# A spectral filter beside an S2-MLP: when the first and third group are turned, and when two layer norms are applied

## The chip, the cores and the metric

The kernel runs on one core of one Trainium2 chip. A core has five engines with a queue each: TensorE (PE in the profile, with its weight loads as PEld) multiplies matrices, VectorE (DVE) and ScalarE (ACT) work elementwise and move results out of PSUM, GpSimd (POOL) works elementwise on data in SBUF, and SyncE (SP) issues the DMA transfers. The metric is device time of one execution in microseconds; the median of several executions counts.

## The reference

`x` is 2048 tokens by 448 channels, `w1` and `w2` are 448 by 448, `w3` is 448 by 1792, `w4` is 1792 by 448, and the spectral weights are 2048 by 225 complex numbers.

```python
def _A_ref(x, w_r, w_i):
    X = rfft2(x, axes=(-2, -1)) * (w_r + 1j * w_i)
    return irfft2(X, s=(S, D), axes=(-2, -1))

def _B_ref(x, w1, w2, w3, w4):
    h = gelu(layernorm(x) @ w1)
    c = D // 4
    g0 = jnp.pad(h[:, :, 0*c:1*c], ((0, 0), (1, 0), (0, 0)))[:, :S, :]   # shift +1
    g1 = jnp.pad(h[:, :, 1*c:2*c], ((0, 0), (0, 1), (0, 0)))[:, 1:, :]   # shift -1
    g2 = jnp.pad(h[:, :, 2*c:3*c], ((0, 0), (2, 0), (0, 0)))[:, :S, :]   # shift +2
    g3 = jnp.pad(h[:, :, 3*c:   ], ((0, 0), (0, 2), (0, 0)))[:, 2:, :]   # shift -2
    hs = jnp.concatenate([g0, g1, g2, g3], axis=-1) @ w2
    x1 = x + hs
    return x1 + gelu(layernorm(x1) @ w3) @ w4

xn = layernorm(x)
return x + _A_ref(xn, w_r, w_i) + _B_ref(xn, w1, w2, w3, w4)
```

Gelu is the tanh form. The MLP branch gets `xn` and normalizes it once more.

## The kernel before

**Data.** The 16 blocks b of 128 rows (`xb(b)`, the tiles xt0 to xt3) lie in four groups of four blocks (`GRP`). The groups are numbered 0 to 3 in the order in which they are worked. Every product of fp32 values is made of three fp16 products: each operand is split into a high part and the remainder (`hi`, `lo`), and hi·hi, hi·lo and lo·hi are summed in PSUM. ACT usually writes the high part, and DVE the low part from it.

**PSUM.** `bank(tag, ...)` gives one of two PSUM banks of each of four tags: "mm", "tr", "acc" and "sp". A bank is free again when its last reader is done.

**First phase, 0 to about 75 us.** The steps for a group g are these.

- `norm1(g, engines)` takes mean and variance (L309, L310) and a first estimate of the reciprocal root on DVE (L333 to L338), and applies both to the four blocks in place (L345 on ACT or L348 on the engine named in the list, one entry per block). It returns `refine` and `scales`, small POOL instructions (L356 to L376) that make the exact per-row scales; `gsc` is needed by the gelu.
- `T1(g)` turns the group: for each of four column tiles t, `turn_pe` transposes four 128 by 128 pieces on PE into one bank (L396), and `turn_copy` writes the high (L406, ACT) and low part (L407, DVE) to `xT`.
- `w1_in` multiplies with w1 (L446; 11 products of 448 columns per block, a block being called a unit here), and `w1_unit` takes the gelu (L465, ACT), splits it into `hs` (L466 ACT, L467 DVE) and has SP transpose it by DMA into `h` (L470).
- `w2_tile(b)` multiplies the shifted pieces of h with w2 (L486; 12 products) and adds to x with L488 on DVE.
- `ln2(blocks, engines, pins)` is the second layer norm: statistics on DVE, the subtraction of the mean (L509 on ACT or L511 on the engine named), a reciprocal root from small DVE instructions, the split into hi (L519, ACT) and lo (L520 and L522, DVE) in a stage tile `y`, and a DMA transpose on SP (L524) into `x2mem`, from where the third layer reads.

The weights w1, w2, w3 and w4 are scaled by powers of two (`powers`: sums of squares by L243 on ACT, L248 on DVE, one product L254, L256 to L261 on DVE) and split. For w3 the split is eight pairs of L284 (ACT) and L285 (DVE). The raw w3 comes by SP (L218); its last quarter is issued behind the eighth h transpose of group 1. The raw w4 (L229) is loaded by SP into space of `x2mem`.

**Main phase.** `mlp` runs eight unit groups G of 256 rows, each with seven pairs fp: `front` (L417 products with w3, gelu L731, split L733 on ACT and L734 on DVE) and `back` (L753 products with w4). Between them stand the steps of the spectral branch. `do_fold` loads two blocks of x, normalizes them on ACT (L548) and folds them on POOL (L554, L557). `step1_in` splits the fold (L564 ACT, L565 DVE), and `step1` multiplies (L574). Then come the column transform, the weights (`wc`, loaded at L619), and the inverse.

**What sets the order.** A scheduler fixes the order of instructions on each engine from the program, the dependences and its own timing model. `behind(key)` adds an order by hand: the instructions within it are issued behind those recorded under the key in `after`. `LATE` gives the pair (G, fp) behind whose split the instructions of the last `ln2` stand, `FOLD` and `PACE` do so for folds and step1, and `WMAX` for maxima over the spectral weights.

Of the kernel before, what the change touches and what calls it, by code (L numbers as in the profile page):

```python
# [13 lines left out]
F16 = mybir.dt.float16  # L14
# [5 lines left out]
S, D, DF, F = 2048, 448, 225, 1792  # L20
# [3 lines left out]
CS = {b: 4 * g + i for b, (g, i) in WHERE.items()}  # L24
PASS = ((0, 0), (0, 1), (1, 0))
SHIFT = [1, -1, 2, -2]
WARM = 25
ZPRE = 2.0 ** -7
UPRE = 2.0 ** -3
VPRE = 2.0 ** -3  # L30
# [3 lines left out]
FOLD = [(0, 5), (1, 0), (1, 1), (1, 3), (1, 4), (1, 6), (2, 0), (2, 2)]  # L34
PIN = [("a3",), ("a3",), ("a3",), ("a3",)]
WMAX = [(1, 4), (1, 5), (1, 6), (2, 0), (2, 1), (2, 2), (2, 3), (2, 4)]
LATE = [(0, 6), (0, 6), (1, 2), (1, 2)]
HS = 3
INV, LAG = 4, 2
EVAC, FILL = 0, 100000  # L40
# [81 lines left out]
def body(tc, nc, x, wf, w1, w2, w3, w4, c_g, c_n, c_small, out):  # L122
    V, A, P, T, SY = nc.vector, nc.scalar, nc.gpsimd, nc.tensor, nc.sync
# [28 lines left out]
    def bank(tag, name):  # L152
        return ps.tile([128, 512], F32, tag=tag, bufs=2, name=name)
# [10 lines left out]
    def xb(b):  # L164
        g, i = WHERE[b]
        return xt[g][:, i]
# [4 lines left out]
    def stage(name, n, side, dtype=F32):  # L171
        t = pw.tile([128, 1808], F32, tag=f"stage{side}", bufs=1, name=name)
        return (t if dtype is F32 else t.bitcast(dtype))[:, :n]
# [11 lines left out]
    wsrc = pc.tile([128, 512], F16, name="wsrc")  # L185
# [195 lines left out]
    after = {}  # L381

    @contextlib.contextmanager
    def behind(*key):
        key = key if len(key) > 1 else key[0]
        with contextlib.ExitStack() as st:
            for i in after[key]:
                st.enter_context(tc.issue_after(i))
            yield

    def turn_pe(g, t):
        pt = bank((("mm", "mm", "tr", "tr") if g == 2 else ("tr", "tr", "acc", "acc"))[t], f"pta{g}{t}")
        w = 128 if t < 3 else 64
        with behind("T", g) if ("T", g) in after else contextlib.nullcontext():
            for i, b in enumerate(GRP[g]):
                m = T.transpose(pt[:w, 128 * i:128 * i + 128], xb(b)[:, 128 * t:128 * t + w], ident)  # L396
        after["T", g] = (m.ins,)
        return pt[:w]
# [11 lines left out]
    def T1(g, ts=range(4)):  # L410
        for t in ts:
            turn_copy(g, t, turn_pe(g, t))
# [11 lines left out]
    w1p = p1.tile([128, 8, D], F16, name="w1p")  # L424
# [15 lines left out]
    def w1_in(g, units, ts, passes=range(3)):  # L440
        for p in passes:
            for t in ts:
                for i, pm in units:
                    wi, xi = ((0, 0), (0, 4), (4, 0))[p]
                    if t < 3 or p != 1:
                        T.matmul(pm[:, :D], xTs[g][:, xi + t, 128 * i:128 * i + 128], w1p[:, wi + t],  # L446
                                 start=t == 0 and p == 0, stop=t == 3 and p == 2)

    hs_buf = [p1.tile([128, 2, 4, 128], F16, name=f"hs{i}") for i in range(HS)]
    for t in hs_buf:  # L450
# [5 lines left out]

    def w1_unit(g, i, pm=None):
        if pm is None:
            pm = bank(("tr" if g == 1 else "mm", "acc")[i // 2], f"pw1_{g}{i}")
            w1_in(g, [(i, pm)], range(4))  # L460
        c = CS[GRP[g][i]]
        pm = pm[:, :D]
        pv_ = pm.rearrange("p (k n) -> p k n", k=4)
        h = hs_buf[c % (HS if g == 3 else HS + 2)]
        A.activation(out=pm, in_=pm, func=AF.Gelu_apprx_tanh, scale=gsc[:, c:c + 1])  # L465
        u = A.activation(out=h[:, 0, :, 0:112], in_=pv_, func=AF.Copy, scale=h1)  # L466
        v = V.scalar_tensor_tensor(out=h[:, 1, :, 0:112], in0=pv_, scalar=h1, in1=h[:, 0, :, 0:112],  # L467
                                   op0=ALU.mult, op1=ALU.subtract)
        o = h_at(g, i)
        d = SY.dma_start_transpose(out=hT[g][:, :, o:o + 128], in_=h.rearrange("p i k n -> p (i k n)"))  # L470
        after[g, i] = u.ins, v.ins
        after["h", g, i] = (d.ins,)
# [18 lines left out]
    def ln2(bs, engines, pins=None):  # L491

        n, b0 = len(bs), bs[0]
        mv = stats([xb(b) for b in bs], f"b{b0}")
        a = pc.tile([128, 4], F32, tag="vb", bufs=2, name=f"vb{b0}")[:, :n]
        r = pc.tile([128, 4], F32, tag="vs", bufs=2, name=f"vs{b0}")[:, :n]
        o, y = [], []
        nm = pc.tile([128, 4], F32, tag="nm", bufs=2, name=f"nm{b0}")[:, :n]
        P.tensor_scalar(out=nm, in0=mv[:, :n, 0], scalar1=-1.0, scalar2=None, op0=ALU.mult)
        for m in range(0, n, 2):  # L500
            w = stage(f"y{b0 + m}", 8 * 448, (b0 + m) // 2 % 2, F16)
            o.append(w[:, 0:4 * D].bitcast(F32).rearrange("p (i n) -> p i n", i=2))
            y.append(w[:, 4 * D:8 * D].rearrange("p (i n) -> p i n", i=2))
            for i in range(2):
                e = engines[m + i]
                c = nm[:, m + i:m + i + 1]
                if e is A:
                    with behind("f", *pins[m + i]) if pins else contextlib.nullcontext():
                        A.activation(out=o[-1][:, i], in_=xb(b0 + m + i), func=AF.Identity, bias=c)  # L509
                else:  # L510
                    e.tensor_scalar(out=o[-1][:, i], in0=xb(b0 + m + i), scalar1=1.0, scalar2=c,  # L511
                                    op0=ALU.mult, op1=ALU.add)
        V.tensor_scalar(out=a, in0=mv[:, :n, 1], scalar1=eps12, scalar2=None, op0=ALU.add)
        rsqrt(r, a, n, f"b{b0}")
        for i in range(n):
            b, h, x_ = b0 + i, y[i // 2][:, i % 2], o[i // 2][:, i % 2]
            k = r[:, i:i + 1]
            with behind("f", *pins[i]) if pins else contextlib.nullcontext():
                u = A.activation(out=h[:, 0:D], in_=x_, func=AF.Copy, scale=k)  # L519
                V.scalar_tensor_tensor(out=h[:, 448:512], in0=x_[:, 384:448], scalar=k, in1=h[:, 384:448],  # L520
                                       op0=ALU.mult, op1=ALU.subtract)
                v = V.scalar_tensor_tensor(out=h[:, 512:896], in0=x_[:, 0:384], scalar=k, in1=h[:, 0:384],  # L522
                                           op0=ALU.mult, op1=ALU.subtract)
            d = SY.dma_start_transpose(out=x2all[:, b // 4][:, :, 128 * (b % 4):128 * (b % 4) + 128], in_=h)  # L524
            after[f"b{b0}"] = u.ins, v.ins, d.ins
# [196 lines left out]
    acc, hs, rest = {}, {}, {}  # L722
# [62 lines left out]
    wps = bank("mm", "wps")  # L785

    def warm_up(n):
        for i in range(n):
            T.matmul(wps, wsrc[:, 0:128], wsrc, start=True, stop=True)

    def warm_rows(n):
        for i in range(n):
            for h, to in ((0, wps), (64, wps2)):
                T.matmul(to, wsrc[h:h + 64, 0:128], wsrc[h:h + 64], start=True, stop=True)

    wps2 = bank("mm", "wps2")
    warm_up(12)
    warm_rows(1)
    warm_up(2)
    warm_rows(2)  # L800
    warm_up(WARM - 21)
    m1, m2, m3, m4 = (pc.tile([128, n], F32, name=f"m{i}") for i, n in ((1, 4), (2, 1), (3, 4), (4, 7)))
    junk4 = row().bitcast(F16)[:, :2 * D]
    V.memset(m1, 0.0)
# [1 line left out]
    xTs = {}  # L806
# [27 lines left out]
    n1 = [norm1(0, [P, V, V, A], mid=squares1)]  # L834
    with behind("n", 0):
        s1, r1 = powers(m1, 4, "1", "mm")
    with behind("p1"):
        pts = [turn_pe(0, t) for t in range(4)]
    h_alloc(0)
    first = [bank("mm" if k < 2 else "sp", f"pw1_0{k}") for k in range(4)]  # L840
    hi, low = split_w(w1p[:, 0], w1p[:, 4], w1s[:, 0], s1, high=V)
    for t in range(4):
        with behind("w1", t - 1):
            turn_copy(0, t, pts[t])
        with behind("a0", t):
            after["w1", t] = split_w(w1p[:, t], w1p[:, 4 + t], w1s[:, t], s1, P if t > 1 else V) if t else (hi, low())
    h1 = pc.tile([128, 1], F32, name="h1")
    V.tensor_scalar(out=h1, in0=s1, scalar1=2.0 ** -5, scalar2=None, op0=ALU.mult)
    for t in range(4):
        w1_in(0, list(enumerate(first)), [t])  # L850
    with behind("ws"):
        n1[0][0]()
    with behind("w1", 1):
# [14 lines left out]
    V.tensor_scalar(out=s12[:, 2:3], in0=s12[:, 0:1], scalar1=s12[:, 0:1], scalar2=EPS, op0=ALU.mult, op1=ALU.mult)  # L868
    p12, eps12 = s12[:, 1:2], s12[:, 2:3]
    with behind("a1"):  # L870
        w1_unit(0, 0, first[0])
        n1.append(norm1(2, [P, V, A, P], 1))
    with behind("a1"), behind("n", 2):
        for k in range(1, 4):
            w1_unit(0, k, first[k])
    with behind("na", 2):
        for k in (1, 3):
            split_w(w2p[:, 0, k], w2p[:, 1, k], w2s[:112, k], s2[:112], P)
    h_alloc(1)
    for k in range(4):  # L880
        w1_unit(1, k)
    T1(2)
    with behind("h", 1, 3):
        load_w3([3])
    n1[2][0]()
    with behind("np", 2):
        n1[0][1]()
    for n in n1[1:]:
        n[1]()
    with behind("a2"):  # L890
        n1 = [norm1(3, [P, P, P, P])]
    h_alloc(2)
# [63 lines left out]
    for i in range(4):  # L956
        P.memset(xh_buf[i][:, 904:], 0.0)
    mlp([1, 2], ahead=AH, tags=("mm", "tr"))
    ln2(range(12, 16), [P, A, P, A], LATE)
    for b in range(0, NB, 2):  # L960
        do_fold(b)
        step1_in(b)
        step1_in(b + 1)
        with behind("m", *PACE[b // 2]):
            step1(b)
            step1(b + 1)
    with behind("X", 14):
        wm = w_scale()
    close("pfd")
# [62 lines left out]
```

## Time and profile before

| | |
|---|---|
| median of 3 runs | 415.83 us (415.5 to 415.83) |
| the profiled execution | 416.13 us |
| its span, first to last instruction | 414.3 us |
| granted TensorE clock | 0.999 |
| PE busy | 407.0 us of the span, 3309 instructions |
| DVE, ACT, POOL busy | 301.2, 245.8 and 115.9 us |
| largest groups of products | L417 149.1 us, L753 138.0 us, L486 39.8 us, L446 35.0 us |

The profile shows one execution. Times are microseconds from the span's start unless a row says otherwise. The list of groups gives busy time and the mean of one instruction for each line of the kernel. A timeline row gives the start, the length of the stretch, engine, line, operation, output and inputs, shapes, the number of instructions in it (x16), and in brackets the idle time ahead of it and what ended that. For SP the length is that of the issuing, and a DMA lands later; "DMA to landing" gives minimum, median and maximum for the rows of one line.

### The profile page before, as it was taken

What the parts mean: (1) busy time and instruction counts of PE and PEld (TensorE: products, weight loads), DVE (VectorE), ACT (ScalarE), POOL (GpSimd) and SP (SyncE); (2) the same over time, 40 slices, a digit from 0 to 9 for tenths busy, and PEclk for the clock granted to TensorE, in tenths of its full rate; (3) what the DMA queues carried; (4) which work ended last, traced back from release to release, by engine and by line L of the source; (5) the groups of instructions that cost most, each with busy time, mean ns of one, the idle gap of its engine ahead of it and who ended that gap; (6) DMA issues with size and microseconds to landing.
All of it is one profiled execution on the core that took longest, in us unless ns stands there. A gap on an engine that the chain in (4) does not pass through costs nothing.

```text
span 414.3 us, 8527 instructions
## 1 busy us (share of the span) xinstructions
PE 407.0 (98%) x3309; PEld 289.4 (70%) x3309; DVE 301.2 (73%) x636; ACT 245.8 (59%) x425; POOL 115.9 (28%) x206
## 2 busy tenths in 40 slices
PE   8999999999999999999999999999999999999996
PEld 3655555765667677776888788787777776677885
DVE  5998999798775867752688889865777687667122
ACT  4588969964649765642578888864444334342321
POOL 2797720101046647400032121210212221221000
PEclk9999999999999999999999999999999999999999
DMA  8959798804931565215056665620000213224001
GB/s 282 349 184 189 148 170 319 162 37 94 219 91 45 134 221 181 91 46 140 14 129 168 152 162 142 147 70 10 2 0 2 68 31 126 90 67 134 24 0 46
DMA packets 53496, 48.53 MB, mean 117 GB/s; under 512 B 37600, under 2 KB 48480, under 8 KB 53456
## 3 DMA queue, kind: packets, MB, share of 16 engines
q1 hardware_dynamic: 53456, 47.99, 43.0%
q8 instruction: 26, 0.43, 0.4%
q14 instruction: 14, 0.11, 0.1%
HBM read 35.52 MB, written 3.67 MB: 95 GB/s over the span
## 4 chain that ended last, share of the span: by engine, by line
PE 88%; DVE 6%; ACT 2%; DMA 2%; issue 1%; POOL 0%
PE pw L417 31%; PE acc L753 30%; PE pw L486 9%; PE pw L446 4%; PE pu L676 3%; PE ps L574 2%; PE pe L696 2%; PE pp L631 2%; PE px L648 2%; PE py L718 2%; DVE sta L309 1%; DMA xt<-x 1%; DMA h<-hs 1%; DVE xT L407 1%; ACT xf L548 1%
## 5 line engine op out<-in xcount | busy, mean ns | idle before, releaser
L417 PE MATMUL pw<-x2mem,w3p 128*128 128x256 f16 x1232 | 149.1, 273 | 0.0
L753 PE MATMUL acc<-w4p,hf 128*128 128x448 f16 (+1 forms) x714 | 138.0, 341 | 0.0
L417 PEld LDWEIGHTS <-w3p 128*128 128x128 f16 x1232 | 118.6, 98 | 18.9
L753 PEld LDWEIGHTS <-hf 128*128 128x128 f16 x714 | 69.4, 98 | 48.5 <-DVE hf L734 0.3
L731 ACT ACTIVATE pw<-pw,pe 128x512 f32<-128x512 f32 x56 | 36.8, 657 | 68.5 <-PE pw L417 68.5
L734 DVE SCALAR_TENSOR_TENSOR hf<-pw,h,hf 128x512 f16<-128x512 f32 x56 | 41.9, 748 | 42.9 <-ACT hf L733 42.5
L486 PE MATMUL pw<-w2p,h 112*128 112x448 f16 x192 | 39.8, 352 | 0.9 <-DMA h<-hs 0.9
L733 ACT ACTIVATE hf<-pw,h 128x512 f16<-128x512 f32 x56 | 38.2, 684 | 1.2
L657 POOL TENSOR_TENSOR z<-te 128x450 f32<-128x450 f32 x16 | 16.3, 1018 | 74.0 <-DVE te L655 74.0
L446 PE MATMUL pw<-w1p,xT 128*128 128x448 f16 x176 | 35.0, 352 | 0.1
L703 POOL TENSOR_TENSOR e<-e 128x226 f32<-128x226 f32 x16 | 11.3, 708 | 77.6 <-ACT e L700 74.7
L486 PEld LDWEIGHTS <-h 112*128 112x128 f16 x192 | 18.6, 98 | 17.0 <-DMA h<-hs 1.1
L446 PEld LDWEIGHTS <-xT 128*128 128x128 f16 x176 | 17.1, 98 | 16.2 <-DVE xT L407 0.4
L638 ACT ACTIVATE pf<-pp 64x450 f16<-64x450 f32 x32 | 17.3, 541 | 16.6 <-DVE pf L639 8.1
L700 ACT ACTIVATE e<-pe 128x452 f32<-128x452 f32 x16 | 8.8, 548 | 26.6 <-PE pe L696 26.5
L639 DVE TENSOR_TENSOR pf<-pp,pf 64x450 f16<-64x450 f32 x32 | 19.9, 622 | 5.3 <-ACT pf L638 5.0
L653 ACT ACTIVATE te<-px 64x450 f32<-64x450 f32 x32 | 17.2, 539 | 0.5
L557 POOL TENSOR_TENSOR f<-xr 128x452 f32<-128x452 f32 x16 | 16.9, 1078 | 0.6
L711 DVE TENSOR_TENSOR vh<-e,vh 128x448 f16<-128x448 f32 x16 | 10.0, 625 | 9.7 <-ACT vh L710 9.7
L554 POOL TENSOR_TENSOR xr<-xf 128x452 f32<-128x452 f32 x8 | 9.1, 1137 | 24.9 <-issue 24.2
L705 DVE TENSOR_TENSOR e<-e 128x113 f32<-128x113 f32 x16 | 9.5, 594 | 7.8 <-POOL e L703 7.8
L565 DVE TENSOR_TENSOR xh<-f,xh 128x452 f16<-128x452 f32 x16 | 12.8, 842 | 2.0 <-ACT xh L564 2.0
(173 smaller groups left out, 604.2 us busy)
## 6 DMA issues: line engine op xcount, KB each, us to landing
wc<-wf SPq DMA_DIRECT2D x32, 225.0 KB, 3.7
wl<-wf SPq DMA_DIRECT2D x8, 450.0 KB, 4.0
xf<-x SPq DMA_DIRECT2D x8, 448.0 KB, 4.1
xt<-x SPq DMA_DIRECT2D x3, 896.0 KB, 12.6
w3raw<-w SPq DMA_DIRECT2D x3, 896.0 KB, 15.7
xr<-x SPq DMA_DIRECT2D x12, 224.0 KB, 2.5
out<-xr SPq DMA_DIRECT2D x12, 224.0 KB, 2.0
gn<-c_g SPq DMA_DIRECT2D x16, 128.0 KB, 3.3
```

The lines of the kernel that those rows point to most:

```text
L417: T.matmul(ps_out, wp[:, wi + t, cols], xT[:, xi + t, tok], start=t == 0 and wi + xi == 0, stop=t == 3 and wi == 4)
L446: T.matmul(pm[:, :D], xTs[g][:, xi + t, 128 * i:128 * i + 128], w1p[:, wi + t], start=t == 0 and p == 0, stop=t == 3 and p == 2)
L486: T.matmul(pm[:, :D], hT[g][:112, 4 * hi + k, o:o + 128], w2p[:, wi, k], start=n == 0, stop=n == 11)
L557: P.tensor_tensor(out=f[:, :, k:k + 2].rearrange("p b s d -> p s b d"), in0=u[:, :, 0], in1=u[:, :, 1], op=op)
L638: A.activation(out=hi, in_=src, func=AF.Copy)
L639: V.tensor_tensor(out=lo, in0=src, in1=hi, op=ALU.subtract)
L653: A.activation(out=e[64 * h:64 * h + 64], in_=px_[64 - 64 * h:128 - 64 * h, :2 * DF], func=AF.Copy)
L657: P.tensor_tensor(out=z, in0=t[:, 0], in1=t[:, 1], op=ALU.add)
L731: A.activation(out=pm, in_=pm, func=AF.Gelu_apprx_tanh, scale=r3)
L733: i = A.activation(out=h[:, 0], in_=pm, func=AF.Copy, scale=h3)
L734: j = V.scalar_tensor_tensor(out=h[:, 1], in0=pm, scalar=h3, in1=h[:, 0], op0=ALU.mult, op1=ALU.subtract)
L753: m = T.matmul(to, h[:, hi, o:o + 128], w4p[0][:, wi, f, r], start=f == 0 and n == 0, stop=f == 13 and n == 2)
```

## The change

There are four edits and one that follows from them.

1. The warm-up products of PE are 23 full ones. Before they were 18 full ones and six on half the rows.
2. The first group is turned in two halves: turns 0 and 1, then the first four products with w1 (pass 0 of tile 0), then turns 2 and 3 behind these products, then the other products.
3. For the third group (g = 2), one block that POOL normalized goes to DVE. All evacuations of group 0, the gelu of its first unit too, are issued behind DVE's applies for group 2. The products of three units of group 1 come ahead of the turns 0 and 1 of group 2; then the fourth unit's products, then turns 2 and 3. The turn banks of group 2 are "mm" and "sp" instead of "mm" and "tr", and the copies of the turns are issued ahead of the evacuations of units 1 to 3 of group 1. The POOL refinements stand behind POOL's applies.
4. `ln2` of blocks 12 to 15 subtracts on ACT alone, stands in the program behind the folds and step1, and its instructions are pinned behind pairs (2, 2) to (2, 5) instead of (0, 6) and (1, 2).
5. With pins, both pairs of `ln2` use the same one of the two stage tiles.

```diff
-WARM = 25
+WARM = 23
-LATE = [(0, 6), (0, 6), (1, 2), (1, 2)]
+LATE = [(2, 2), (2, 3), (2, 4), (2, 5)]
...
-        pt = bank((("mm", "mm", "tr", "tr") if g == 2 else ("tr", "tr", "acc", "acc"))[t], f"pta{g}{t}")
+        pt = bank((("mm", "mm", "sp", "sp") if g == 2 else ("tr", "tr", "acc", "acc"))[t], f"pta{g}{t}")
...
-            pm = bank(("tr" if g == 1 else "mm", "acc")[i // 2], f"pw1_{g}{i}")
+            pm = bank(("mm", "acc")[i // 2], f"pw1_{g}{i}")
...
-            w = stage(f"y{b0 + m}", 8 * 448, (b0 + m) // 2 % 2, F16)
+            w = stage(f"y{b0 + m}", 8 * 448, 0 if pins else (b0 + m) // 2 % 2, F16)
...
-    warm_up(12)
-    warm_rows(1)
-    warm_up(2)
-    warm_rows(2)
-    warm_up(WARM - 21)
+    warm_up(WARM)
...
-        pts = [turn_pe(0, t) for t in range(4)]
+        pts = [turn_pe(0, t) for t in range(2)]
...
     for t in range(4):
+        if t == 1:
+            after["T", 0] = (w1_in(0, list(enumerate(first)), [0], [0]).ins,)
+            pts += [turn_pe(0, 2), turn_pe(0, 3)]
         with behind("w1", t - 1):
             turn_copy(0, t, pts[t])
...
     for t in range(4):
-        w1_in(0, list(enumerate(first)), [t])
+        w1_in(0, list(enumerate(first)), [t], range(0 if t else 1, 3))
...
     with behind("a1"):
-        w1_unit(0, 0, first[0])
-        n1.append(norm1(2, [P, V, A, P], 1))
+        n1.append(norm1(2, [P, V, A, V], 1))
     with behind("a1"), behind("n", 2):
-        for k in range(1, 4):
+        for k in range(4):
             w1_unit(0, k, first[k])
     with behind("na", 2):
         for k in (1, 3):
             split_w(w2p[:, 0, k], w2p[:, 1, k], w2s[:112, k], s2[:112], P)
     h_alloc(1)
-    for k in range(4):
-        w1_unit(1, k)
-    T1(2)
+    second = [bank(("tr", "acc")[k // 2], f"pw1_1{k}") for k in range(4)]
+    for k in range(3):
+        after["w1m", k] = (w1_in(1, [(k, second[k])], range(4)).ins,)
+    with behind("na", 2):
+        w1_unit(1, 0, second[0])
+    for k in range(2):
+        if k:
+            with behind("T", 2):
+                after["w1m", 3] = (w1_in(1, [(3, second[3])], range(4)).ins,)
+        with behind("w1m", 2 + k):
+            T1(2, [2 * k, 2 * k + 1])
+        with behind("a2"):
+            w1_unit(1, 1 + k, second[1 + k])
+    with behind("a2"):
+        w1_unit(1, 3, second[3])
     with behind("h", 1, 3):
         load_w3([3])
-    n1[2][0]()
     with behind("np", 2):
-        n1[0][1]()
-    for n in n1[1:]:
-        n[1]()
+        n1[2][0]()
+        for n in n1:
+            n[1]()
...
     mlp([1, 2], ahead=AH, tags=("mm", "tr"))
-    ln2(range(12, 16), [P, A, P, A], LATE)
     for b in range(0, NB, 2):
         do_fold(b)
         step1_in(b)
...
             step1(b + 1)
+    ln2(range(12, 16), [A] * 4, LATE)
```

`w1_in` now returns its last product and takes a list of passes, so that `after` can hold it.

More of the change, by code (lines that the diff above doesn't have):

```diff
@@ L445, in w1_in @@
                     if t < 3 or p != 1:
-                        T.matmul(pm[:, :D], xTs[g][:, xi + t, 128 * i:128 * i + 128], w1p[:, wi + t],
-                                 start=t == 0 and p == 0, stop=t == 3 and p == 2)
+                        m = T.matmul(pm[:, :D], xTs[g][:, xi + t, 128 * i:128 * i + 128], w1p[:, wi + t],
+                                     start=t == 0 and p == 0, stop=t == 3 and p == 2)
+        return m
     hs_buf = [p1.tile([128, 2, 4, 128], F16, name=f"hs{i}") for i in range(HS)]
@@ L789, in warm_up @@
             T.matmul(wps, wsrc[:, 0:128], wsrc, start=True, stop=True)
[L791 to L796, printed above, removed]
-    warm_up(12)
-    warm_rows(1)
-    warm_up(2)
-    warm_rows(2)
-    warm_up(WARM - 21)
+    warm_up(WARM)
     m1, m2, m3, m4 = (pc.tile([128, n], F32, name=f"m{i}") for i, n in ((1, 4), (2, 1), (3, 4), (4, 7)))
```

## The prediction

> **What bounds the kernel now.** I read the header, the busy line and the chain of waits first, then the list of waits by releaser, then busy time by stage.
>
> ```profile
> span 414.3 us, 8527 instructions
> PE 407.0 (98%) x3309; PEld 289.4 (70%) x3309; DVE 301.2 (73%) x636; ACT 245.8 (59%) x425; POOL 115.9 (28%) x206
> PE 88%; DVE 6%; ACT 2%; DMA 2%; issue 1%; POOL 0%
> ```
>
> TensorE (PE) is busy 407.0 of 414.3 us. The change takes no product away, so all it can win is idle time of PE, and all it can lose is new idle time. The sum below is made against the profiled execution: 416.13 us, a span of 414.3 and 1.83 around it. That is 0.30 above the median of 415.83, and I take 0.3 off at the end. The list of waits names the holes that this change can touch:
>
> ```profile
> PE pw L486 <- DMA h<-hs: 0.9, 1, 0.9
> PE ps L574 <- DVE xh L565: 1.0, 2, 0.7
> ```
>
> (Idle us, how often, longest.) The first is at 33 us, where a second-layer product waits for a transposed h. The second is at 136 us, where step1 of the third fold waits for its split halves. Both are small. What is not small is what the stages look like on the other engines:
>
> ```profile
> 46.00:58.00 12.00, 12.00 (x66) 6.34 (x65) 11.61 (x38) 8.59 (x16) 7.85 (x20) 1.00 0.77 138
> 58.00:70.00 12.00, 12.00 (x65) 6.21 (x64) 11.97 (x20) 12.00 (x17) 0.00 (x0) 1.00 0.97 309
> 126.00:138.00 12.00, 11.10 (x90) 7.96 (x87) 8.06 (x9) 11.21 (x22) 9.91 (x10) 1.00 0.28 69
> ```
>
> (Stretch, length, then busy PE, weight load, DVE, ACT, POOL, the granted clock, DMA share, GB/s.) From 46 to 70 PE is full, but DVE is too: 11.61 and 11.97 of 12. There DVE has no room, and whatever the change puts later in its queue comes out later. The clock is full everywhere.
>
> **The change part by part.** *Warm-up.* 23 products for 24 in another shape; the first work behind them waits for the sum of squares of w1, not for PE. Nothing.
>
> *First turn.* Two of the four turns of group 0 (8 of 16 transposes) go behind the first four products.
>
> ```profile
> 9.75 1.95 PE L396 MATMUL pta<-ident,xt 128*128 128x128 f32 x16
> 10.42 1.08 ACT L406 ACTIVATE xT<-pta 128x512 f16<-128x512 f32 x2 [0.67 <-PE pta L396]
> 11.53 8.49 PE L446 MATMUL pw<-w1p,xT 128*128 128x448 f16 x44
> 19.85 0.28 PE L254 MATMUL pw<-pt,ones 128*128 128x1 f32 x2
> 20.25 1.97 PE L396 MATMUL pta<-ident,xt 128*128 128x128 f32 x16
> ```
>
> 16 transposes take 1.95, so 8 end issue near 10.7; the first copy ends near 11.0 (10.42 and half of 1.08), a few tenths later for its signal. PE now idles 0.3 to 0.5 there, where before the other turns covered the copy. It can win back the most of what stands at 19.85: two one-column products (L254, waiting for DVE's sum over w2) hold PE 0.40 until 20.25, some 0.3 of it idle, and DVE's sum comes sooner when half the copies are behind. I take +0.1, bounds -0.3 and +0.5.
>
> *Third turn.* Group 2 is turned before the last unit of group 1 is multiplied. A unit is 11 products of 0.19 (8.49/44), so PE asks for the turned x 2.1 us sooner than the 30.86 of the first row here.
>
> ```profile
> 30.86 0.49 PE L396 MATMUL pta<-ident,xt 128*128 128x128 f32 x3
> 28.91 0.51 DVE L348 TENSOR_SCALAR xt<-xt,vy,nma 128x448 f32<-128x448 f32 x1
> 29.34 1.27 DVE L467 SCALAR_TENSOR_TENSOR hs<-pw,h,hs 128x448 f16<-128x448 f32 x2
> 33.33 1.31 PE L486 MATMUL pw<-w2p,h 112*128 112x448 f16 x6 [0.85 <-DMA h<-hs]
> ```
>
> The transposes need the applies (L348; one of four goes from POOL to DVE, +0.45 on DVE) and two PSUM banks that the two L467 release. L467 now stands behind both applies on DVE. PE asks at 28.8 and gets the first bank near 29.9 to 30.4, so 1.1 to 1.6 idle. In exchange the wait at 33.33, with what lies just before it 1.2 in all, is filled by the unit moved behind the turn. Net +0.2; bounds -1.2 (no new wait) and +0.9. What is behind the applies on DVE, the four L467 and with them the h transposes, comes about 0.5 to 1 later, and so does the issue of the last w3 loads, which SyncE (SP) holds behind the eighth h transpose.
>
> *The side effect that decides.* In the order built for the changed kernel the split of the second layer norm's first pair (y0: L519 on ACT, L520 and L522 on DVE) has moved. Before, DVE did it ahead of the w3 scale; now it stands behind all eight w3 splits (L284 on ACT, L285 on DVE). The first third-layer product needs both y0 transposes.
>
> ```profile
> 49.47 0.61 DVE L522 SCALAR_TENSOR_TENSOR y<-y,vs 128x384 f16<-128x384 f32 x1
> 52.90 0.15 DVE L248 TENSOR_REDUCE pt<-m 128x1 f32<-128x4 f32 x1
> 68.76 1.15 DVE L285 SCALAR_TENSOR_TENSOR w3p<-w3raw,pe,w3p 128x896 f16<-128x896 f32 x1
> 57.70 7.55 ACT L284 ACTIVATE w3p<-w3raw,pe 128x896 f16<-128x896 f32 x8
> 58.12 2.62 SPq L524 DMA_TRANSPOSE x2mem<-y  x2
> 70.51 1.26 PE L417 MATMUL pw<-x2mem,w3p 128*128 128x256 f16 x10
> ```
>
> Before: y0 is split at 50.1, its transposes go at 58.12, PE starts at 70.51 without a wait, and the last L285 has ended at 69.91, 0.6 sooner. DVE needs 17.0 us from L248 (52.90) to that end, at 97 to 100% busy. After: from L248 to y0's last L522 the same work and in addition y0's four instructions (about 1.5: two at 0.61, two short ones) and the small ones of its reciprocal root (about 1.3), less one L488 pair of 0.6 and waits: about 19.1.
>
> L248 itself waits for the fourth sum of squares over w3:
>
> ```profile
> 39.71 1.23 SPq L218 DMA_DIRECT2D w3raw<-w  x2
> DMA to landing us min/median/max: 5.4/6.0/6.6
> 49.90 1.69 ACT L243 ACTIVATE xr<-w3raw 128x1792 f16<-128x1792 f32 x1
> ```
>
> Its loads go 1.7 later by the step above (41.4), land at 48.6 (second issue 0.6 later, then 6.6), and with the square 1.9 the reduction stands at 50.6, 2.3 before its old place, since y0 is no longer ahead of it. 50.6 + 19.1 gives y0 done at 69.7. Against that I set a plain count: with the same waits as before DVE ends at 68.5 (69.9 less 1.3 for instructions that now come later), without any wait after 28 us at 66.6. From above, the second pair, y2, stands at that very place now:
>
> ```profile
> 70.70 2.58 SPq L524 DMA_TRANSPOSE x2mem<-y  x2
> ```
>
> Its second transpose goes at 72.0. I take 69.7, the longer of my two counts, as DVE has hardly waited in this stage.
>
> SP then issues the two transposes at 68.9 and 70.2 (pitch 1.3 from 2.62/2). Landing takes 3.1:
>
> ```profile
> DMA to landing us min/median/max: 2.9/3.1/6.0
> ```
>
> 70.2 + 3.1 = 73.3 against 70.51: **+2.8**. Bounds: 0 (DVE at 66.6, landed by 70.4) and +4.6 (in y2's place, 72.0 + 3.1). While the wait binds, the two parts above it vanish in it: PE only waits the less if it comes later.
>
> *What comes behind that wait.* SP issues the w4 loads behind the y0 transposes:
>
> ```profile
> 60.79 2.21 SPq L229 DMA_DIRECT2D x2mem<-w  x4
> DMA to landing us min/median/max: 5.4/8.5/10.3
> 66.80 0.94 ACT L243 ACTIVATE xr<-x2mem 128x896 f16<-128x896 f32 x1
> 72.74 4.75 PE L417 MATMUL pw<-x2mem,w3p 128*128 128x256 f16 x42
> ```
>
> The loads move from 60.79 to about 71.5 and land from 77 to 83.5. ACT's squares of w4 (L243) stand ahead of the gelu of the first third-layer bank, and the last products of layer two wait on DVE and on h transposes that queue behind those loads. Following ACT I get the first bank free at 81.7 where PE asks at 83.9, covered by 2.2; a w2 bank is 0.3 late. The group-3 h transposes are on time if they share the DMA engines with the loads, and 1.3 late if they wait for them. I take **+0.8**, bounds 0 and 2.5. The landing row rises from 5.4 to 10.3 over the four loads issued 0.55 apart, so the loads are served one after the other. The Trainium skill, "DMA: Bandwidth & Descriptors", section "Queues, rings and completion order", says that on each DMA engine the descriptors of one queue are consumed in ring order; the row agrees. By it this term would be 1.6 and the sum 0.8 higher; if a transpose passed loads, 0 and 0.8 lower.
>
> *Late normalization.* ln2 of blocks 12 to 15 moves behind the fold loop, all on ACT, its splits to the third unit group near 170 to 190 us.
>
> ```profile
> 131.44 1.13 DVE L520 SCALAR_TENSOR_TENSOR y<-y,vs 128x64 f16<-128x64 f32 x1 [0.36 <-ACT y L519]
> 129.43 1.93 POOL L557 TENSOR_TENSOR f<-xr 128x452 f32<-128x452 f32 x2
> 136.05 2.03 DVE L565 TENSOR_TENSOR xh<-f,xh 128x452 f16<-128x452 f32 x2
> 136.72 0.73 PE L574 MATMUL ps<-csm,xh 128*128 128x128 f16 x10 [0.36 <-DVE xh L565]
> 138.13 0.73 PE L574 MATMUL ps<-csm,xh 128*128 128x128 f16 x10 [0.68 <-DVE xh L565]
> ```
>
> The splits at 131 stand ahead of L565 on DVE, and L565 starts at 136.05, though the fold it reads was done at 131.4. Without them it can end near 133 to 134, ahead of PE at 136. PE's holes here, 1.36 with the short ones, go: **-1.36**, bounds -1.5 and 0. At the new place ACT idles 0.8 to 3.3 per unit, and the moved transposes pass these loads on SP:
>
> ```profile
> 188.32 1.15 SPq L619 DMA_DIRECT2D wc<-wf  x2
> ```
>
> The first reader of that stream runs near 204, 8 us behind the landing. I cost the new place at 0; without that cover each transpose pair would cost up to 1.3 on SP, the upper bound 2.6.
>
> Sum: 416.13 + 2.8 + 0.8 - 1.36 = 418.4; less 0.3 is **418.1**.
>
> **The rivals.** *A, the y0 wait does not bind.* DVE has no waits (66.6) or the transposes land before PE asks. Then the sum is 416.13 + 0.1 + 0 - 1.36 - 0.3 = 414.6 (413.7 to 415.5 by the third turn's bounds). For it: PE leaves DVE 0.6 before 70.51 now, and the count gives 66.6 to 68.5. Against it: DVE is at 11.97 of 12, and transposes need 4 us behind it. It decides if y0 ends on DVE before 66.8.
>
> *B, the parts cancel.* y0 is done at 68.0: half the wait (1.1), no queueing behind w4. 416.13 + 1.1 - 1.36 - 0.3 = 415.6.
>
> *C, the w4 loads decide.* The late loads hold ACT's squares, and with these gelu and the second-layer banks. 2.5 instead of 0.8, and the wait at its 3.3: 420.3. For it: DMA is at 0.97 in that stage. Against: 2.2 of cover.
>
> *D, the late part doesn't do what it says.* POOL folds (L557, 9.91 of 12 busy) are the last to arrive, and step1 still waits: 419.5.
>
> **How the numbers follow.** Likeliest 0.54 (own range 416.5 to 419.8), A 0.20, B 0.12, C 0.09, D 0.05. About 0.2%, or 0.83 us, is what a measurement of this kernel can tell from no change, so faster means under 415.0 and slower over 416.66. Faster: most of A, 0.17, and 0.01 of B: 0.18. Same: the rest of A 0.03, B 0.10 and 0.04 of the likeliest: 0.17. Slower: 0.50 of the likeliest, 0.01 of B, C and D: 0.65. The range leaves out half of A below and half of C above: 414.6 to 420.4.
>
> **What would show it.** In the changed profile the first third-layer product should wait for the x2mem<-y transposes near 70 to 73, with y0's last L522 on DVE behind the last L285. L574 at 136 should not wait for L565. The wait at 33 should be gone and a similar one for the turn stand near 29 to 30. A first third-layer product at 70.5 or sooner would make the prediction wrong, and so would new holes of over 2 us in 75 to 95 us, or at 170 to 205.

## The result, and the profile after

The changed kernel takes 420.47 us in the median (420.04 to 421.55, 4 runs), the kernel before 415.66 in the same comparison: a ratio of 1.0121, 95% interval 1.010 to 1.0142. It is 4.8 us slower; 418.1 was predicted, and the upper end of the range, 420.4, is just missed. The profiled execution took 420.26 us. Some executions of these kernels hold a stretch at half clock (last section) and take 1.0 to 1.4 us longer, and the medians below mix both: with early loads, for one, ten executions have a median of 417.85, and the five of them with a mean granted clock of 0.999 or more one of 417.07. The profile's head, busy line and chain of waits, to be set against those of before:

```profile
span 418.5 us, 8524 instructions
PE 407.0 (97%) x3308; PEld 289.6 (69%) x3308; DVE 299.6 (72%) x637; ACT 246.2 (59%) x427; POOL 113.7 (27%) x203
PE 82%; DVE 6%; DMA 5%; ACT 3%; issue 1%; SPq 1%; POOL 0%; ACTq 0%
```

PE does the same 407.0 us of work in a span 4.2 longer: all of the loss is idle time of PE. Three lines of the list of PE's waits after (idle us, times, longest), and the PE timeline rows of the new waits:

```profile
PE pw L487 <- DVE xt L489: 1.7, 1, 1.7
PE pta L396 <- POOL vw L369: 1.6, 1, 1.6
PE pw L417 <- DMA x2mem<-y: 1.3, 1, 1.3
```

```profile
11.14 0.92 PE L446 MATMUL pw<-w1p,xT 128*128 128x448 f16 x4 [0.27 <-ACT xT L406]
30.70 1.20 PE L396 MATMUL pta<-ident,xt 128*128 128x128 f32 x8 [1.56 <-POOL vw L369]
72.27 1.86 PE L487 MATMUL pw<-w2p,h 112*128 112x448 f16 x9 [1.69 <-DVE xt L489]
75.42 3.33 PE L417 MATMUL pw<-x2mem,w3p 128*128 128x256 f16 x29 [1.29 <-DMA x2mem<-y]
90.17 0.74 PE L487 MATMUL pw<-w2p,h 112*128 112x448 f16 x3 [0.41 <-DMA h<-hs]
```

(The lines named here stand one higher than before from L449 on: L487 is the old L486, L489 the old L488, L521 and L523 the old L520 and L522, L575 the old L574, L566 the old L565; in the kernels further down they shift with each edit.) The wait for L565 at 136 us is gone, and so is that for h at 33. The first third-layer product starts at 75.42 and not at 70.51, with the same products of layers one and two ahead of it: 4.9 us lost by then, 0.4 more at 90, 1.4 won at 136. That is nearly all of the 4.1 by which the two profiled executions differ (420.26 and 416.13). The rows on DVE, ACT and SP that hold the first third-layer product:

```profile
52.54 0.16 DVE L248 TENSOR_REDUCE pt<-m 128x1 f32<-128x4 f32 x1 [3.21 <-ACT xr L243]
68.46 1.11 DVE L285 SCALAR_TENSOR_TENSOR w3p<-w3raw,pe,w3p 128x896 f16<-128x896 f32 x1
71.01 0.61 DVE L523 SCALAR_TENSOR_TENSOR y<-y,vs 128x384 f16<-128x384 f32 x1
71.54 0.67 DVE L489 SCALAR_TENSOR_TENSOR xt<-xt,cs,pw 128x448 f32<-128x448 f32 x1
```

```profile
36.57 1.70 ACT L243 ACTIVATE xr<-w3raw 128x1792 f16<-128x1792 f32 x1
38.25 1.15 ACT L467 ACTIVATE hs<-pw,h 128x448 f16<-128x448 f32 x2
50.72 1.70 ACT L243 ACTIVATE xr<-w3raw 128x1792 f16<-128x1792 f32 x1 [3.53 <-DMA w3raw<-w]
```

```profile
37.65 4.81 SPq L471 DMA_TRANSPOSE h<-hs  x3
42.50 2.11 SPq L218 DMA_DIRECT2D w3raw<-w  x2
70.97 2.63 SPq L525 DMA_TRANSPOSE x2mem<-y  x2
```

y0's last L523 stands behind the last L285 and ends at 71.62; its transposes go at 70.97 and about 72.3. The L489 that PE waits for first (1.69) is queued behind y0 on DVE, at 71.54. DVE, which was full here before, now stands idle for 3.21 us in front of L248. ACT waits 3.53 for w3, whose last loads go out 2.8 later (42.50 for 39.71) behind the eighth h transpose.

### The profile page after: what moved, and what is told of

It is laid out like the page before. It is cut to its first block, busy times and chain, and to the rows that moved or that the text cites. A ratio compares the mean times of both kernels' runs of the same rounds, so it can differ in the third digit from the quotient of the medians.

```text
span 418.5 us, 8524 instructions
## 1 busy us (share of the span) xinstructions
PE 407.0 (97%) x3308; PEld 289.6 (69%) x3308; DVE 299.6 (72%) x637; ACT 246.2 (59%) x427; POOL 113.7 (27%) x203
## 4 chain that ended last, share of the span: by engine, by line
PE 82%; DVE 6%; DMA 5%; ACT 3%; issue 1%; SPq 1%; POOL 0%; ACTq 0%
PE pw L417 31%; PE acc L754 30%; PE pw L487 4%; PE pu L677 3%; PE ps L575 3%; PE pe L697 2%; PE pp L632 2%; PE px L649 2%; PE py L719 2%; PE pw L446 2%; DMA h<-hs 2%; DMA w3raw<-w 2%; DVE sta L309 1%; ACT w3p L284 1%; DMA xt<-x 1%
## 5 line engine op out<-in xcount | busy, mean ns | idle before, releaser
L487 PE MATMUL pw<-w2p,h 112*128 112x448 f16 x192 | 39.3, 352 | 2.2 <-DVE xt L489 1.7
L487 PEld LDWEIGHTS <-h 112*128 112x128 f16 x192 | 18.7, 98 | 19.0 <-issue 2.3
L566 DVE TENSOR_TENSOR xh<-f,xh 128x452 f16<-128x452 f32 x16 | 12.8, 842 | 2.0 <-ACT xh L565 2.0
```

What stands on the lines that cost most here:

```text
L487: T.matmul(pm[:, :D], hT[g][:112, 4 * hi + k, o:o + 128], w2p[:, wi, k], start=n == 0, stop=n == 11)
```

## The experiments

| kernel | median us | ratio to before, 95% |
|---|---|---|
| changed kernel | 420.47 | 1.0121, 1.010 to 1.0142 |
| late normalization alone | 414.59 | 0.9972, 0.996 to 0.9983 |
| first turn alone | 416.56 | 1.0024, 1.0014 to 1.0035 |
| third group alone | 427.24 | 1.0267, 1.0245 to 1.0289 |
| changed without first turn | 420.03 | 1.0102, 1.0085 to 1.0119 |
| changed, y0 ahead of the w3 splits | 419.10 | 1.0078, 1.0059 to 1.0097 |
| changed, early w3 loads | 417.85 | 1.0048, 1.0034 to 1.0062 |
| changed, both | 415.88 | 1.0011, 0.9999 to 1.0022 |
| both, without first turn | 415.68 | 1.0002, 0.9991 to 1.0013 |
| changed, y0 ahead of L248 | 421.36 | 1.0125, 1.0101 to 1.0149 |
| both, POOL's w2 splits later | 414.97 | 0.9979, 0.9959 to 0.9998 |
| the last without first turn | 414.76 | 0.9976, 0.9963 to 0.9989 |
| late normalization, late w3 loads | 414.30 | 0.9965, 0.9949 to 0.9981 |
| late normalization, y0 last | 417.76 | 1.0054, 1.0026 to 1.0081 |
| late normalization, both late | 425.69 | 1.0252, 1.0226 to 1.0278 |
| late normalization, gsc first | 414.87 | 0.9980, 0.9967 to 0.9992 |

Medians of the kernel before were 415.6 to 415.9 in these comparisons.

**Each part alone.** First the late normalization in the kernel before (with it goes the shared stage tile, part 5, whose line is as in the change):

```diff
-LATE = [(0, 6), (0, 6), (1, 2), (1, 2)]
+LATE = [(2, 2), (2, 3), (2, 4), (2, 5)]
...
-    ln2(range(12, 16), [P, A, P, A], LATE)
     for b in range(0, NB, 2):
...
+    ln2(range(12, 16), [A] * 4, LATE)
```

> The kernel before with the late normalization alone (part 4 and 5). My theory: the two holes of PE in front of L574 near 136 us (0.52 and 0.84) go and nothing comes in their place, so about 1.3 us faster than before (ratio near 0.997). Rival (the fold on POOL is last to arrive, or the new place at 170 to 190 costs ACT time on the path): within 0.4 us of before, and L574 still waits, or a new hole of PE between 160 and 205 us.

It is 1.3 us faster (0.28%). Its PE timeline at step1:

```profile
136.31 1.39 PE L574 MATMUL ps<-csm,xh 128*128 128x128 f16 x22
```

22 products of step1 run in 1.39 us with no wait in brackets, and from there PE waits no more until 262 us. No version below is clearly faster: the one with late loads has the lowest median, 414.30, and an interval that overlaps.

The third group alone (the diff's hunks for g == 2, the bank tags and the block from `norm1(2, ...)` to `n[1]()`):

> The kernel before with the third group's edit alone (part 3). My theory: the whole loss comes from this part, so about 6.2 us slower than before (4.8 of the whole change and 1.3 that the late part wins there), with y0's L521 and L523 on DVE behind the last L285, and first third-layer product near 75.4 us. Rival (the first turn shares in the loss by what it does to DVE's order): under 5.5 us slower.

427.24: 11.4 us slower, twice what I expected. The holes at 70 to 75 us are those of the changed kernel (1.69 and 1.23); the one at 89 is 1.18 for 0.41. And PE now waits much more at step1, in its list of waits:

```profile
PE ps L575 <- DVE xh L566: 2.5, 4, 1.1
PE ps L575 <- ACT xh L565: 1.3, 2, 1.1
```

```profile
122.53 1.00 DVE L293 TENSOR_SCALAR nib<-vb 128x4 int32<-128x4 int32 x1
123.56 0.98 DVE L294 TENSOR_SCALAR nib<-nib 128x4 int32<-128x4 int32 x1
125.11 0.99 DVE L296 TENSOR_TENSOR nqb<-nib 128x4 f32<-128x4 f32 x1
126.14 0.90 DVE L297 TENSOR_TENSOR nqb<-nqb,vb 128x4 f32<-128x4 f32 x1
127.08 0.16 DVE L298 SCALAR_TENSOR_TENSOR nqb<-nqb 128x4 f32<-128x4 f32 x1
128.12 1.23 ACT L520 ACTIVATE y<-y,vs 128x448 f16<-128x448 f32 x2 [5.69 <-DVE vs L302]
129.26 1.03 ACT L565 ACTIVATE xh<-f 128x452 f16<-128x452 f32 x2
```

The stage is late by the earlier holes. The reciprocal root of the last ln2, in its old place, now falls on the POOL folds: four small DVE instructions take about 1 us each for 0.16. ACT sits 5.69 us at L520 for it, and step1's L565 is queued behind L520. On top of the 3.8 us of waits in the list, the granted clock was 0.50 from 132.4 to 135.8 us (last section), which costs about 1.7 more, an estimate by half of the 3.41 us. So the parts do not add. The counterpart, the changed kernel without the first turn and warm-up parts:

> The changed kernel without parts 1 and 2: third group and late normalization. If the parts add, it stands 1.3 us under the third group alone, 425.9. By the traces they don't: with the third group alone, 6.3 us of new holes stand at step1 between 128 and 150 us, where the old late normalization meets the folds on DVE. So I expect 419.5 to 420.3, the late normalization worth about 7 us here for 1.3 alone.

420.03: with the third group's edit in, moving the late normalization is worth 7.2 us, for 1.3 alone. (The 6.3 us of holes in the expectation take in that stretch at half clock.)

The first turn alone (parts 1 and 2):

> The kernel before with the two halves of the first turn and the full warm-up products alone (parts 1 and 2). My theory: PE idles 0.44 us ahead of the first product, as it does in the changed kernel, and wins back the 0.34 at the second L254, so within 0.4 us of before. Rival (it shares in the loss, since DVE's order around y0 changes too: one of the two y0 splits then stands behind L248): more than 1 us slower, with a hole near 70 us.

0.24% slower, about 0.8 to 1.0 us; no hole near 70, though DVE's order around y0 did change. The two profiled executions differ by only 0.37 (416.50 and 416.13), and the traces explain that much: the first products start 0.14 later, PE idles 0.44 more between the last of the eight transposes and the first product, and 0.26 is won back at the second L254 (the expectation's 0.34 was too much). In context the first turn costs 0.44 (420.47 against 420.03) and 0.2 in two pairs below, all inside the intervals. Where the rest of the 0.8 lies in the kernel alone stays open.

**y0 or the loads?** The changed kernel with one order more, the w3 splits behind y0's:

```diff
             after[f"b{b0}"] = u.ins, v.ins, d.ins
+            after[f"s{b0}"] = u.ins, v.ins
...
-        with behind(*PIN[b - 4]):
+        with behind(*PIN[b - 4]), behind("s0"):
```

> The changed kernel with one order more: the eight w3 splits (L284, L285) go behind y0's splits. Nothing else. Theory A (it is y0's place on DVE that costs): the holes of PE at 70 to 75 us (1.85 and 1.46) and the one at 89.5 (0.57) go, so about 3.5 to 3.9 us faster than the changed kernel, 416.6 to 417.0. Theory B (the late w3 loads cost it whatever the order, since they hold the fourth sum of squares to 52.4 us and all of DVE's work behind it): the first third-layer product still starts over 73 us, and less than 1.9 us is won, 418.6 or more.

419.1: only 1.4 won. The wait for x2mem<-y went and the first third-layer product starts at 70.78, as in theory A; but h transposes and L489 held PE 1.1 and 1.0 us instead, and the win is that of theory B. Here y0's splits (60.3 us) stand ahead of the w3 splits but still behind L248, in front of which DVE idles 3.57 us, so what y0 passed comes late instead. Theory A was too simple. Early loads:

```diff
-    with behind("h", 1, 3):
-        load_w3([3])
...
     with behind("na", 2):
+        load_w3([3])
         w1_unit(1, 0, second[0])
```

> The changed kernel with the loads of w3's last quarter issued behind group 2's applies, ahead of group 1's h transposes, and not behind the eighth of them. y0's place on DVE stays behind the splits. Theory A: L248 comes 2 to 3 us sooner than 52.54 and y0 with it, as DVE's stage behind it stays 19.1 us long; first third-layer product near 73, so 2 to 2.5 us faster than the changed kernel, about 418.2, not the whole loss. Theory B (the loads are the cause): the whole 3.3 us of holes at 70 to 75 go, 417.0. If the loads don't reach DVE (DVE full in any case): no change, 420.4.

417.85: 2.6 won in the median, y0's order unchanged. The profiled execution took 416.75, 3.5 less than that of the changed kernel. In its DVE and PE timelines:

```profile
48.41 0.15 DVE L248 TENSOR_REDUCE pt<-m 128x1 f32<-128x4 f32 x1
67.49 0.62 DVE L523 SCALAR_TENSOR_TENSOR y<-y,vs 128x384 f16<-128x384 f32 x1
```

```profile
72.00 3.44 PE L417 MATMUL pw<-x2mem,w3p 128*128 128x256 f16 x30 [0.43 <-DVE y L523]
```

L248 came 4.1 sooner and y0's end 3.5 sooner (68.11). From L248 to y0's end DVE needs 19.7 us here, 19.1 in the changed kernel. The product starts 3.4 sooner (72.00 for 75.42). With both edits:

> The changed kernel with the early w3 loads and with y0's splits ahead of the w3 splits. Theory B (the late loads are the cause, and y0's place adds the rest): the holes left with the early loads, 0.59 at 71 and 0.50 at 86 us, go too, so about 1 us under the kernel with early loads alone, 416.8. Rival (DVE is full in this stage, so what y0 wins the w2 sums L489 or the h splits lose, as with y0 first alone): within 0.4 us of 417.85.

> The same two edits without the halved first turn and with the old warm-up: third group, late normalization, early w3 loads and y0 ahead. If the first turn costs what its hole shows (0.44 less 0.34), this is within 0.4 us of the kernel with both edits. If a halved first turn costs more through DVE and ACT, it is 0.5 to 1 us faster than that. Whatever is left over the late normalization alone (414.59) is the price of the third group's turn, by the hole of 1.4 to 1.7 at 28.8 us less the 1.2 at 33 us that goes: 0.2 to 0.5 us by this sum, so about 415.0.

415.88 and 415.68. Together the edits win 4.6. What is left over the late normalization alone, 1.3 with the first turn and 1.1 without it, is the price of the turns; no hole of PE over 0.2 us is left between 40 and 240 us. The first turn is worth 0.2 here, inside the intervals.

Then y0 ahead of the fourth square and of L248, by moving `powers` for w3 behind `ln2([0, 1])`:

```diff
...
+    with behind("s0"):
+        squares(m3[:, 3:4], w3raw[:, 3])
+        s3, r3 = powers(m3, 4, "3", "mm")
```

> The changed kernel with y0's splits ahead of the fourth sum of squares on ACT and of L248 on DVE, as they stand in the kernel before; the w3 loads stay late, behind the eighth h transpose. Theory C (DVE sits blocked at L248 for 3.2 us, waiting for the late loads, with y0's work queued behind it; before, that work filled the wait): with y0 ahead the late loads cost nothing, the holes at 70 to 75 and at 89 us go, and the time is that of the kernel with both edits, 415.9 (up to 416.5). Theory B (late loads shift all DVE work of the stage): at least half of the 3.9 us of holes stays, 418 or more.

421.36, over theory B's 418, but the run tells nothing of theory C (and its trace holds a stretch at half clock, from 80.8 to 84.2). The order changed elsewhere: on ACT two sums of squares of w4 came ahead of the w3 splits and waited for w4's loads, so the splits began at 68.09 for 57.54.

```profile
66.07 0.95 ACT L243 ACTIVATE xr<-x2mem 128x896 f16<-128x896 f32 x1 [3.72 <-DMA x2mem<-w]
68.09 7.56 ACT L284 ACTIVATE w3p<-w3raw,pe 128x896 f16<-128x896 f32 x8
```

So the question goes to the kernel with the late normalization, without the third group's edit, as a table of two by two. Late loads:

```diff
-    with behind("h", 1, 3):
-        load_w3([3])
...
         w1_unit(2, k)
+        if k == 0:
+            with behind("h", 2, 0):
+                load_w3([3])
```

> The kernel before with the late normalization, and with the loads of w3's last quarter one h transpose later on SP (behind the first of group 2), which makes them about 6 us late, 45.8 for 39.71. Here y0 stays ahead of the w3 scale on DVE. Theory A (late loads hurt only as y0 waits behind them): L248 is 1 to 2 us late, the first third-layer product still starts near 70.5, and the time is within 0.7 us of the late normalization alone, 414.6. Theory B (the late loads hurt by themselves, through all of DVE's stage): 1.5 us or more slower, over 416.1.

y0's splits behind the w3 splits, by a call of `w3_block`, which holds the w3 splits, in the midst of `ln2([0, 1])`; without and with the late loads. In both, six sums of squares of w4 that stood among the w3 splits stand behind them:

```diff
+            with behind("f", *pins[i]) if pins else behind("w3s") if mid else contextlib.nullcontext():
...
+    ln2([0, 1], [A, P], mid=w3_block)
```

> The kernel before with the late normalization, and with y0's splits ordered behind the eight w3 splits; w3's loads where they were (39.7). Neither the first nor the third group's turn is changed. Theory D (it takes both: y0 behind the splits, and w3 loads so late that DVE's 19 us of work behind L248 ends too late): L248 comes near 50, y0 ends 19 us behind it near 69, a hole of 0.5 to 2.5 us ahead of the first third-layer product; 415.1 to 417.1. If y0's place is all, the whole 3.3 to 3.9: 418 or more. If it is nothing without the third group: 414.6.

> As the last, and w3's last loads one h transpose later (45.1), which alone cost nothing. Theory D: L248 near 53.8, y0 done near 73, first third-layer product at 76 to 77, so 4 to 6 us over the late normalization alone: 418.5 to 420.6. If the two don't act together (the loss comes from something else in the third group's edit), no more than the kernel with y0 last, within 1 us.

| | loads at 39 us | loads at 45 to 46 us |
|---|---|---|
| y0 ahead of L248 | 414.59 | 414.30 |
| y0 behind the w3 splits | 417.76 | 425.69 |

Late loads alone cost nothing, y0 last alone costs 3.2, both measure 11.1 more than neither. Theory D's sizes did not hold: 417.76 lies between its 417.1 and the 418 of its rival, and 425.69 far above its 420.6. Rows of DVE and PE, first of the kernel with late loads alone, then with y0 last alone, then with both:

```profile
53.84 0.16 DVE L248 TENSOR_REDUCE pt<-m 128x1 f32<-128x4 f32 x1 [0.27 <-ACT xr L243]
69.92 1.15 PE L417 MATMUL pw<-x2mem,w3p 128*128 128x256 f16 x9
```

```profile
50.00 0.16 DVE L248 TENSOR_REDUCE pt<-m 128x1 f32<-128x4 f32 x1 [0.18 <-ACT xr L243]
73.43 8.79 PE L417 MATMUL pw<-x2mem,w3p 128*128 128x256 f16 x79 [1.29 <-DMA x2mem<-y]
```

```profile
55.32 0.16 DVE L248 TENSOR_REDUCE pt<-m 128x1 f32<-128x4 f32 x1 [1.19 <-ACT xr L243]
75.95 0.62 DVE L524 SCALAR_TENSOR_TENSOR y<-y,vs 128x384 f16<-128x384 f32 x1
79.79 2.51 PE L417 MATMUL pw<-x2mem,w3p 128*128 128x256 f16 x11 [4.33 <-DVE nqb L298]
```

With y0 ahead, L248 may be at 53.8 and the first third-layer product stands at 69.9. With y0 last the product hangs on L248 + 20 to 21 us of DVE + a transpose. The last cell shows that late loads do cost when y0 stands last, but not how much, since other things changed in it too. A transposed x of the fourth group came late, and PE waited 2.76 for it ahead of 57.16; L254, behind that wait on PE, then kept DVE idle for 2.11 at 61 us. The splits of the second pair, y2, came ahead of the w3 splits (62.66). And behind the 4.33 us of waiting the granted clock was 0.50 from 79.5 to 82.9. The product starts 6.4 later than with y0 last alone (L248 is 5.3 later), and the profiled executions differ by 8.4 (425.48 and 417.12).

**The turn of the third group.** PE waits 1.56 ahead of it. This edit goes for what makes the applies late:

```diff
-        for k in (2, 0):
-            after["w2p"] = split_w(w2p[:, 0, k], w2p[:, 1, k], w2s[:112, k], s2[:112], high=P)
...
         n1.append(norm1(2, [P, V, A, V], 1))
+    with behind("np", 2):
+        for k in (2, 0):
+            after["w2p"] = split_w(w2p[:, 0, k], w2p[:, 1, k], w2s[:112, k], s2[:112], high=P)
```

> The kernel with early w3 loads and y0 ahead of the w3 splits, and with POOL's splits of w2's first two tiles behind its apply for group 2. In the kernels so far DVE's small L333 and L335 take 0.98 and 0.89 us, for 0.16 elsewhere, while POOL runs L276. Theory (POOL's two-input work holds DVE up): they fall to about 0.16, the applies come 1.5 us sooner and the hole before the third group's turn falls from 1.6 to under 0.4 us; about 1 us under 415.88, if w2's tiles still come in time (else a new wait of up to 1 us at 36 us). Rival (the turn waits for its banks, not for the applies): hole as before, 415.9.

> The third group's edit and the late normalization with all three mends: early w3 loads, y0 ahead of the w3 splits, POOL's w2 splits behind its apply; and without the halved first turn. By the holes of PE (0.44 for the first turn, less 0.34) 0.1 to 0.4 us under 414.97, so 414.6 to 414.9, no better than the late normalization alone at 414.59.

414.97 and 414.76. DVE rows of the changed kernel with POOL's beside them, then DVE rows of the first of these two kernels:

```profile
26.34 0.98 DVE L333 TENSOR_SCALAR va<-mva 128x4 f32<-128x4 f32 x1
27.43 0.89 DVE L335 TENSOR_SCALAR vy<-va 128x8 int32<-128x8 int32 x1
26.26 2.02 POOL L276 TENSOR_TENSOR w2p<-w2s,w2p 112x448 f16<-112x448 f32 x2
```

```profile
28.36 0.17 DVE L333 TENSOR_SCALAR va<-mva 128x4 f32<-128x4 f32 x1
28.63 0.17 DVE L335 TENSOR_SCALAR vy<-va 128x8 int32<-128x8 int32 x1
```

The hole ahead of the turn, from start to start of products, fell from 1.6 to 0.2, and waits at 36 us rose from 0.3 to 0.8. Whether PE had waited for the applies or for the banks stays open: the L468 that free the banks are queued behind the applies on DVE, and came sooner with them. With all its mends the third group's edit ends where the late normalization alone stands (414.76 and 414.59): the new turn wins nothing that shows.

Last, a try to better the late normalization, with `gsc` of group 1 ahead of the w2 splits on POOL:

```diff
         n1[1][0]()
+    with behind("gsc", 1):
         for k in (2, 0):
```

> The kernel before with the late normalization, and POOL's scales of group 1 (gsc, L365) ahead of its w2 splits (L274 to L276) and not behind them. ACT waited 1.55 us for gsc at 28.7; the gelus of group 1 and with them the h transposes come 1 to 1.5 us sooner, so the hole of PE at 32 us (0.3 to 1.0) goes: 0.3 to 0.8 us under the late normalization alone, 413.8 to 414.3. Rival: the h transposes wait on SP or DVE in any case (DVE L467 behind the applies), hole and time as without, 414.6.

414.87, no better: the rival holds, the hole stayed (0.96 ahead of the product at 33.14 in the profiled run).

## Why the prediction was right and wrong

- *The side and the place* were right: the loss is PE's wait at the third layer, made by y0's new place behind the w3 splits. The two by two table shows that this place costs by itself (3.2 us), and the two edits to the changed kernel that y0's place and the late loads together make up 4.6. Not foreseen: 1.69 of the idle time there is a wait for L489, queued behind y0 on DVE, and 1.29 the wait for y0's transposes.
- *The stage on DVE* was right: 19.1 us from L248 to y0's end were predicted, 52.54 to 71.62 are 19.1.
- *Its start was mis-sized*, and that is the failure: "the reduction stands at 50.6". It stood at 52.54, so y0 ended at 71.6 for 69.7, and the product started at 75.4 for 73.3: +4.9 and not +2.8. I had the loads go at 41.4. They went at 42.50, because ACT took a sum of squares of w3 (36.57, 1.70 long) ahead of the last two high parts of h (38.25), and SP needed 4.81 for three h transposes; the issue of the two loads also took 2.11 for 1.23. That they came late I had seen, and the sum has all of y0's work behind L248. The plain counts that I set against it (66.6 and 68.5) do not: they leave out the 3.21 us that DVE stood idle in front of L248 with that work in its queue.
- *"I take 69.7, the longer of my two counts"*: the bound that I had read from y2's place (second transpose at 72.0) was within 0.3 of what happened. That is in part luck: it goes from an L248 at 52.90, and L248 came back to 52.54 for another reason, the late loads. Had it stood at 50.6, 19.1 us of DVE would have ended at 69.7, as I reckoned.
- *First turn*: 0.3 to 0.5 idle were predicted, the trace shows 0.44. Its price of +0.1 may be low: 0.2 to 0.4 in context, inside the intervals, and 0.8 to 1.0 alone.
- *Third turn*: 1.1 to 1.6 idle were predicted, 1.56 came; the wait at 33 went. As predicted, its lateness vanishes in the later wait, which the DVE chain sets.
- *Behind y0*: +0.8 was predicted. About 0.4 at 90 us came, for h transposes queued behind the w4 loads, as argued. Transposes did not pass the loads: the two of y2, issued at 76.05 and 78.53 behind them, landed 9.6 and 7.9 us later, where 3.1 is the median.
- *Late normalization*: -1.36 predicted, -1.3 measured alone (414.59 for 415.87), the new place at no cost.
- *Rivals*: A and B did not come, as DVE did not gain; C's price was near the time, but its mechanism was not what held PE; D fell.

In sum the profiled execution was forecast at 418.4 and took 420.26, 1.9 too low, which is about the error in L248.

## What to carry to other kernels

Here the work that DVE did while it waited for a load was free, and the same work queued behind that load was not: check for each late transfer what stands behind its first reader. A term that hangs on a chain of five queues (ACT, SP, DMA, ACT, DVE) deserves a wide range: two steps of it, each about 1 us off, moved the time by 2. A part of a change was worth 1.3 us alone and 7 us beside another part, so prices add only if the order they meet is the same.

## What the runs showed of the hardware

- Some small DVE instructions take 0.9 to 1.0 us for 0.16 while POOL runs work on large tiles (L276 above, the folds at 122 us). The Trainium skill, "SBUF — State Buffer", section "Who interferes with whom", says that DVE and GpSimd share a port pair as an exclusive lock, so that where both need it the other blocks for a whole instruction; the rows agree: 0.98 is about one L276 of 1.01. Four of the nine small instructions of a reciprocal root lost 3.2 us so, at 122 us with the third group alone.
- A window in which PE idled for half the time halved its clock. Seven times in the seventeen traces the granted clock falls to 0.50 inside the kernel, each time for 3.41 us. With each trace cut into steps of 3.41 us from there, PE idled 1.73 to 3.41 us in the seven windows just ahead of a fall, and at most 1.69 us in every other one between 2 and 405 us. The idle time need not be in one piece: ahead of the second pair here no hole is over 1.14. Pairs of windows (length, busy PE, weight load, DVE, ACT, POOL, granted clock, DMA share, GB/s), of the late normalization alone, of the third group alone, and of the changed kernel, where 1.69 idle left the clock at 1.00:

```profile
7.38:10.79 3.41, 1.62 (x14) 1.34 (x13) 2.54 (x10) 2.42 (x6) 1.16 (x2) 1.00 1.00 336
10.79:14.20 3.41, 3.41 (x14) 1.99 (x13) 3.37 (x8) 3.10 (x7) 2.49 (x6) 0.50 1.01 276
128.99:132.40 3.41, 1.61 (x20) 1.14 (x21) 3.41 (x8) 1.90 (x4) 0.00 (x0) 1.00 0.38 76
132.40:135.81 3.41, 3.41 (x22) 2.61 (x20) 1.52 (x3) 1.32 (x3) 0.00 (x0) 0.50 0.34 66
70.50:73.91 3.41, 1.72 (x10) 0.78 (x8) 3.41 (x8) 1.42 (x3) 0.00 (x0) 1.00 0.45 87
73.91:77.33 3.42, 2.13 (x20) 1.75 (x19) 3.42 (x10) 0.00 (x0) 0.00 (x0) 1.00 0.95 243
```

  In the first pair five products took 0.37 for 0.19, and about 0.9 us was lost. This early fall comes and goes from run to run with the warm-up products. Their first row in the kernel before, then two rows of the late normalization alone:

```profile
1.22 5.30 PE L789 MATMUL wps<-wsrc 128*128 128x512 f16 x12 [1.22 <-DVE wsrc L186]
1.22 4.10 PE L789 MATMUL wps<-wsrc 128*128 128x512 f16 x12 [1.22 <-DVE wsrc L186]
9.48 0.35 PE L254 MATMUL pm<-pt,ones 128*128 128x1 f32 x2 [1.79 <-DVE pt L248]
```

  L254 starts at nearly the same time in both (9.53 and 9.48), but the warm-up ends at 9.16 in one and at 7.69 in the other, so PE idles 0.38 and 1.79 us in between. The Trainium skill, "TensorE: Matmul & The Clock Gate", section "What's actually happening", names an idle window of about 3.4 us; here a window of that length that was half idle was enough.
